# First batch's coarse softmax scaled inside its transposing matmul, second batch's sums moved from GpSimd to VectorE, and new queue orders

## The chip, the cores and the metric

The kernel runs on one core of a Trainium2 chip. The metric is the device time of one execution in microseconds, taken as the median of several runs. Engines are named as in the profile: PE is TensorE (PEld its weight loads), DVE is VectorE, ACT is ScalarE, POOL is GpSimd, SP is SyncE, which issues the DMAs.

## The reference

Four batches of 576 positions go through three stages: a two-scale attention, a block with a two-dimensional Fourier transform and an MLP, and a gated output block.

```python
# attention, per batch and head (8 heads, head size 64, factor 4, S = 576, Sd = 144)
out_d = sm_attn(q_d, k_d, v_d)            # q_d.. are means over groups of 4 positions
out_up = np.repeat(out_d, 4, axis=2)      # the coarse part, "base" in the kernel
mask = np.abs(pos[:, None] - pos[None, :]) < 4
scores = np.where(mask, 0.125 * q @ k.T, -1e9)
out_local = softmax(scores) @ v
x = out_up + out_local                    # reshaped to (4, 576, 512)
# Fourier and MLP
u = x + real(fft(fft(x, axis=1), axis=2))
un = (u - mean) / sqrt(var + 1e-6)
y = u + relu(un @ w_ch1) @ w_ch2          # 512 -> 2048 -> 512
# gate
gate = sigmoid(5-tap causal convolution of y along the sequence)
out = (gate * (y @ w_val)) @ w_out
```

## The kernel before, in words

Features lie on partitions and positions on the free axis: a batch's `X` is 128 x 4 x 576 (four feature blocks). The MLP and the gate work in 12 units of 192 positions (`UT`), three to a batch. Products of the main part are split into a high and a low float16 half (`uh`, `ul`, `hh`, `hl`), three matmul passes for one product; unit (0, 0) alone runs in float32 (`steps32`, tiles `u`, `h`), from weights as they arrive.

The weights arrive as 64-bit floats. For each piece of 1024 columns, DVE builds the float32 words in three integer operations (`word_op`, tiles `W`, `raw`), later ACT and DVE split them into halves (`conv_w`).

`chain0` is the head of the program: the attention and Fourier stage of batch 0. Its names in the rows are: `dS` scores of the local attention, `dmx` their maxima, `dP` the exponentials, `dsu` their sums, `dPT` and `PT` the transposed probabilities, `dO` the local output; `qkT` the pooled q and k, `sc` the coarse scores of a head pair, `nm` their maxima, `E` the coarse exponentials, `lsu` their sums, `eT` and `ET` the transposed probabilities, `po` and `base` the coarse output; `cv`, `tr`, `ss_v` and `tot` a norm of v; `fF`, `FH`, `FL` the folded sequence and its halves, `ab`, `AH`, `AL` the first Fourier product, `pp`, `pq`, `DS` the second. `mir` is a mirrored copy. The head ends with `u`, the centred input of unit (0, 0); the first matmul of the MLP (`ph` from `u`, line 1160) waits for it. Batches 1 to 3 do the same stage in `attn_steps`, spread between the units of the batch before; batch 1 needs its result at the fourth unit.

The coarse step of `chain0` for one head pair is `coarse` (PE), `coarse_max` (DVE), `coarse_exp` (ACT), `coarse_norm` (the sum plus 1e-9 and its reciprocal on DVE, then the product of the exponentials with it on GpSimd), `coarse_turn` (eight 72 x 72 transposes on PE into `eT`, a copy to `ET` on ACT) and `coarse_value`.

The order of the work is fixed by hand: `ORDER` lists, for SP and the four engines, in which sequence the numbered steps of the program (`parts`) stand in that engine's queue, and each queue runs strictly in that order. `SLOT` says which buffer of a ring each tile takes. `EN_G`, `XB_G` and the expressions in `attn_steps` choose between GpSimd and another engine for single operations.

Of the kernel before, what the change touches and what calls it, by code (L numbers as in the profile page):

```python
# [9 lines left out]
F32 = mybir.dt.float32  # L10
# [9 lines left out]
SD = S // 4  # L20
# [34 lines left out]
0 2 1 4 7 3 5.0 11 5.1 6 13 9 8 14 10 15.2 12 15.1 16.0 15.3-4 195.1 16.1 15.0 119.2 15.5 119.3 185.0 123.1 16.2 119.0  # L55
123.0 119.1 122.1 195.0 122.0 171 172.0 170 174 172.1 173 211.1 211.0 229.1 229.0 185.1 230.1 185.2 230.0 284 308.1
285 309.1 288.1 262.0 288.0 262.1 310.0 262.2 289.1 289.0 271 309.0 308.0 359 324 360.0 310.1 360.1 310.2 361.1 361.0
420.1 341 362.1 345 362.0 386.1 386.0 421.0-1 377 386.2 403 472.0 419.0 472.1 421.2 420.0 419.1 459 475 476 477.1 446
477.0 487 512.1 547 512.0 512.2 532 528 565 606 595 625 654 664 687 690 691
""",  # L60
    "gpsimd": """
0.0 5 48.1 48.0 54 71 85 136.1 136.0 137 139.1 139.0 0.1 195.1 195.0 195.2 183.0-1 183.3 183.2 193 211.1 211.0 229
211.2 217.0-1 217.3 230.1 217.2 230.0 230.2 231 241.1 241.0 249 255 259.1 259.0 267 269 272.1 272.0 274.1 274.0 275
277.0 286.0-2 283.0 286.3 283.1-5 290.0 283.6 290.1 283.7 290.2 283.8 121 278.0 290.3 286.4 277.1 318 278.1 339 359.1
325.1 325.0 390.0 359.0 337 307 359.2 360.1 360.0 361.1 361.0 360.2 361.2 390.1 362 390.2-3 395 398 404.0 408.1 408.0
407.1 407.0 404.1 411 428.1 428.0 434.0 417 414.1 414.0 434.1 483.0-1 472.1 472.0 472.2 451 475.1 475.0 475.2 476
# [50 lines left out]
197.8 213.0 209 197.15 204 210 197.16 193.2 214 219 215 212 213.2 213.1 220 216.0-2 250 251 221 216.3-4 216.9-10 216.5
216.11 216.6-7 222 216.8 216.12 217 236.0-1 216.13-16 224 231.0 225 231.3-5 231.1-2 236.2 226 252.1 257 252.0 236.3
# [1812 lines left out]
```

## Time and profile before

| | before |
|---|---|
| median of 3 runs | 667.07 us (666.96 to 668.61) |
| the profiled execution, its own time | 668.18 us |
| its span, first to last instruction | 666.4 us |
| PE busy | 647.4 us, 97% of the span |
| PE weight loads busy | 581.6 us |
| DVE busy | 458.3 us, 69% |
| ACT busy | 328.5 us, 49% |
| POOL busy | 127.1 us, 19% |
| mean granted TensorE clock | 0.985 of full speed |

The time of an execution is the span and some 1.8 us around it. A busy PE is not PE at its peak, since matmuls overlap one another; a clock of 0.50 in a row is TensorE at 1.2 GHz, one of 1.00 is 2.4 GHz.

### The profile page before, as it was taken

The numbers are of one execution on the slowest core, as the hardware profiler recorded it, in microseconds if no ns is written. First come the engines' busy times: TensorE is split into PE (matmuls) and PEld (weight loads), VectorE is DVE, ScalarE is ACT, GpSimd is POOL, SyncE is SP. The second block draws the span as 40 slices with busy tenths as digits, with TensorE's granted clock in tenths as the row PEclk, the third lists the DMA queues.
The fourth block names the chain that finished last, engine by engine and source line by source line (L and its number), as shares of the span: only waits on it lengthen the run. The fifth ranks groups of instructions, "written<-read, shape, count | busy, mean of one in ns | idle before, by whom it ended". The sixth has DMA issues, their size and how long they took to land.

```text
span 666.4 us, 18165 instructions
## 1 busy us (share of the span) xinstructions
PE 647.4 (97%) x7751; PEld 581.6 (87%) x7751; DVE 458.3 (69%) x950; ACT 328.5 (49%) x997; POOL 127.1 (19%) x178
## 2 busy tenths in 40 slices
PE   8968999999999999999999999999999999999997
PEld 4647799999998887989988898998999989999895
DVE  3679999989998877657876645675447763562344
ACT  3665577888334757675235576643232313312122
POOL 0240306321210613501110352030001020000000
PEclk9959999999999999999999999999999999999999
DMA  8976072313424001403240020000300000000001
GB/s 301 402 247 243 2 253 82 101 34 100 161 60 171 20 18 46 142 1 104 77 150 2 27 62 17 3 1 25 116 2 17 2 1 33 1 2 18 2 32 48
DMA packets 23299, 52.08 MB, mean 78 GB/s; under 512 B 1855, under 2 KB 11071, under 8 KB 22194
## 3 DMA queue, kind: packets, MB, share of 16 engines
q1 hardware_dynamic: 23218, 50.91, 22.4%
q8 instruction: 61, 1.00, 0.6%
q14 instruction: 20, 0.16, 0.1%
HBM read 44.41 MB, written 8.26 MB: 79 GB/s over the span
## 4 chain that ended last, share of the span: by engine, by line
PE 78%; DVE 11%; issue 5%; DMA 3%; POOL 2%; ACT 1%; SPq 0%; POOLq 0%; ACTq 0%
PE ph L1196 25%; PE pc L1216 24%; PE out L1324 7%; PE val L1308 7%; DVE W L448 5%; PE ab L996 2%; POOL E L451 1%; PE dO L805 1%; PE po L1572 1%; PE st L1080 1%; PE sc L883 1%; DMA raw<-in_moe_w_ch_dram 1%; PE pc L1171 1%; DMA kTa<-in_k_dram 1%; PE dPT L788 1%
## 5 line engine op out<-in xcount | busy, mean ns | idle before, releaser
L1196 PE MATMUL ph<-uh,W 128*128 128x192 f16 x1408 | 198.3, 246 | 1.3 <-DVE hl L448 0.7
L1196 PEld LDWEIGHTS <-W 128*128 128x128 f16 x2112 | 176.8, 98 | 9.5 <-issue 4.3
L1216 PE MATMUL pc<-hh,W 128*128 128x192 f16 x1232 | 171.7, 246 | 0.0
L1196 PE MATMUL ph<-ul,W 128*128 128x192 f16 x704 | 171.2, 246 | 0.0
L1216 PEld LDWEIGHTS <-W 128*128 128x128 f16 x1848 | 154.3, 98 | 5.7 <-issue 1.4
L1216 PE MATMUL pc<-hl,W 128*128 128x192 f16 x616 | 129.5, 246 | 0.0
L1200 ACT ACTIVATE hh<-ph 128x384 f16<-128x384 f32 x88 | 42.7, 488 | 125.8 <-PE ph L1196 100.5
L448 DVE SCALAR_TENSOR_TENSOR hl<-ph,hh 128x384 f16<-128x384 f32 x88 | 48.2, 552 | 77.6 <-ACT hh L1200 77.4
L448 DVE SCALAR_TENSOR_TENSOR W<-X,cw,W 128x192 f32<-128x192 f32 x160 | 64.1, 437 | 2.7 <-ACT W L1271 2.3
L1308 PE MATMUL val<-yy,W 128*128 128x192 f16 x576 | 59.6, 246 | 0.5 <-ACT yy L1250 0.5
L1308 PEld LDWEIGHTS <-W 128*128 128x128 f16 x576 | 48.5, 98 | 1.1 <-issue 0.4
L1324 PE MATMUL out<-W,gh 128*128 128x512 f16 x144 | 46.5, 379 | 0.0
L769 ACT ACTIVATE dP<-dS,dmx 128x64 f32<-128x64 f32 x120 | 36.2, 329 | 0.6 <-PE dPT L788 0.3
L448 DVE SCALAR_TENSOR_TENSOR W<-W,W 128x1024 int32<-128x1024 int32 x24 | 29.5, 1237 | 0.1
L451 POOL TENSOR_TENSOR E<-E,lsu 72x288 f32<-72x288 f32 x16 | 18.9, 1197 | 55.1 <-ACT nm L1529 19.7
L454 POOL TENSOR_TENSOR sq<-sq 128x384 f32<-128x384 f32 (+1 forms) x12 | 10.6, 880 | 93.6 <-ACT sq L1091 93.2
L1324 PE MATMUL out<-W,gl 128*128 128x512 f16 x72 | 27.1, 379 | 0.0
L769 ACT ACTIVATION_READ_ACCUMULATOR dP<-dS,dmx 128x1 f32 x120 | 26.7, 223 | 0.0
L1324 PEld LDWEIGHTS <-gh 128*128 128x128 f16 x144 | 14.0, 98 | 12.0 <-issue 0.2
L1216 PE MATMUL pc<-hh,Wz 128*128 128x192 f16 x176 | 24.3, 246 | 0.0
L1171 PE MATMUL pc<-h,W 128*128 128x192 f32 x128 | 23.3, 329 | 0.0
L1160 PE MATMUL ph<-u,W 128*128 128x192 f32 x128 | 22.5, 327 | 0.4 <-DVE u L1711 0.4
(288 smaller groups left out, 1212.0 us busy)
## 6 DMA issues: line engine op xcount, KB each, us to landing
W<-in_moe_w_ch_dram SPq DMA_DIRECT2D x12, 1024.0 KB
out_dram<-osb SPq DMA_DIRECT2D x17, 256.0 KB
vw<-in_vw_dram SPq DMA_DIRECT2D x8, 512.0 KB
v<-in_vp_dram SPq DMA_DIRECT2D x24, 144.0 KB
X<-in_q_dram SPq DMA_DIRECT2D x6, 576.0 KB
kT<-in_k_dram SPq DMA_DIRECT2D x4, 582.0 KB
X<-in_moe_w_ch_dram SPq DMA_DIRECT2D x2, 1024.0 KB
raw<-in_moe_w_ch_dram SPq DMA_DIRECT2D x4, 512.0 KB
```

The source lines that it names most:

```text
L448: return eng.scalar_tensor_tensor(out=out, in0=in0, scalar=scalar, in1=in1, op0=op0, op1=op1)
L451: return eng.tensor_tensor(out=out, in0=a, in1=b, op=ALU.mult)
L454: return eng.tensor_tensor(out=out, in0=a, in1=b, op=ALU.add)
L769: A.activation(out=s_[:, z, a], in_=pss[par][:, z, a], func=AF.Exp, scale=SCALE, bias=mx[:, par, z, a:a + 1], accum_out=su[:, par, z, a:a ...
L996: T.matmul(out=ps[0:n, c0:c1], lhsT=d[x][:, c, sd, e, n0:n0 + n], rhs=feat[:, w, c, c0:c1], start=(t == 0), stop=(t == 5),)
L1160: T.matmul(out=ps[:, e], lhsT=W[AT[kc * 2 + m // 8] + 1][:, o:o + 128], rhs=u()[:, kc, :], start=(kc == 0), stop=(kc == 3))
L1171: T.matmul(out=c["ps"][m // 2][:, m % 2], lhsT=W[9 + g][:, o:o + 128], rhs=hs[g // 2][:, g % 2, e, :], start=(kk == 0 and m % 2 == 0), sto ...
L1196: T.matmul(out=ps[:, e], lhsT=w1_ap(pw, kc, 2 * g + e), rhs=uh[px][:, kc, :], start=(t == 0), stop=(t == 11))
L1200: A.activation(out=h_, in_=ps, func=AF.Relu)
L1216: T.matmul(out=ps[m // 2][:, m % 2], lhsT=w2_ap(pw, kk, m), rhs=x[px][:, e, :], start=(kk == 0 and (pw, px) == (0, 0) and m % 2 == 0), sto ...
L1308: T.matmul(out=ps[:, e], lhsT=wv_ap(pw, kc, 2 * mh + e), rhs=m_["y"][px][:, kc, :], start=(t == 0), stop=(t == 11))
L1324: T.matmul(out=ps, lhsT=(gh, gl)[px][:, kc, t * 128:(t + 1) * 128], rhs=wo_ap(pw, kc), start=(n == 0), stop=(n == 11))
```

## The change

Six things change.

1. `coarse_norm` of batch 0 no longer multiplies the exponentials on GpSimd. DVE builds, for each head pair and head, a 72 x 2 x 72 tile `dg`: the unit matrix with the reciprocal sums on its diagonal. `coarse_turn` multiplies by it in a plain float32 matmul where it transposed by the unit matrix. Eight DVE operations take the place of eight GpSimd operations.
2. `EN_G` is empty: batch 1's coarse exponentials are scaled by ACT (16 operations of 72 x 144) where GpSimd did it in 8.
3. `XB_G` is gone: two base additions of batch 1 go from GpSimd to DVE.
4. Batch 1's two differences `fs` and its four far-half additions (`X<-X,DS`, 128 x 287) go from GpSimd to DVE.
5. The tile `busy`, whose products fill waits of PE at the start, shrinks to 128 x 128 and is read four times over for the same 512 columns.
6. `ORDER` is new for all five queues, and `SLOT` for two rings; of both a line or two stand below.

```diff
-EN_G = (1,)
+EN_G = ()
-XB_G = ((1, 1), (1, 3))
...
-    busy = const.tile([P, 512], F16, name="busy")
+    busy = const.tile([P, P], F16, name="busy")
...
-                add(G if (b, a) in XB_G else V, x[:, a], x[:, a], d["base"][:, a].unsqueeze(2).to_broadcast([P, SD, 4]))
+                add(V, x[:, a], x[:, a], d["base"][:, a].unsqueeze(2).to_broadcast([P, SD, 4]))
...
-                    (V, G)[sd].tensor_tensor(
+                    (V, G)[sd * (b > 1)].tensor_tensor(
...
-                add(G, X[:, c, b0:b1], X[:, c, b0:b1], DS[:, 1, HALF - 2:0:-1])
+                add(V if b == 1 else G, X[:, c, b0:b1], X[:, c, b0:b1], DS[:, 1, HALF - 2:0:-1])
...
-                add(G, X[:, c + 2, b0:b1], X[:, c + 2, b0:b1], DS[:, 0, HALF - 2:0:-1])
+                add(V if b == 1 else G, X[:, c + 2, b0:b1], X[:, c + 2, b0:b1], DS[:, 0, HALF - 2:0:-1])
...
             for par in range(2):
-                mul(G, E[:, par], E[:, par], s_[:, par].unsqueeze(2).to_broadcast([QC, 2, SD]))
+                lr["dg", a, par] = sp.tile([QC, 2, QC], F32, tag="dg", name="dg", bufs=3)
+                mul(V, lr["dg", a, par], eye[0:QC, 0:QC].unsqueeze(1).to_broadcast([QC, 2, QC]),
+                    s_[:, par].unsqueeze(2).to_broadcast([QC, 2, QC]))
...
-                        T.transpose(out=pe[:, kc, qc], in_=lr["E", a][:, par, qc, kc * QC:(kc + 1) * QC],
-                                    identity=eye[0:QC, 0:QC])
+                        T.matmul(out=pe[:, kc, qc], lhsT=lr["E", a][:, par, qc, kc * QC:(kc + 1) * QC],
+                                 rhs=lr["dg", a, par][:, qc], start=True, stop=True)
```

The first place where the order moves is DVE's queue in the head, just ahead of the first `dsu` of the two large groups of local scores. Before, after the last reciprocal of `lsu`, it reads:

```order
L1540 RECIPROCAL lsu<-lsu 72x4
L547 TENSOR_SCALAR W_114<-X 128x1024
L547 TENSOR_SCALAR W_115<-W_123 128x1024
L448 SCALAR_TENSOR_TENSOR W_114<-X,W_114 128x1024
L448 SCALAR_TENSOR_TENSOR W_115<-W_123,W_115 128x1024
L547 TENSOR_SCALAR W_116<-W_119 128x1024
L448 SCALAR_TENSOR_TENSOR W_114<-X,W_114 128x1024
L448 SCALAR_TENSOR_TENSOR W_116<-W_119,W_116 128x1024
L1467 TENSOR_SCALAR dsu<-dsu 128x16
```

Now:

```order
L1548 RECIPROCAL lsu<-lsu 72x4
L523 TENSOR_REDUCE f_v_565<-tot 128x1
L459 TENSOR_TENSOR dg<-eye,lsu 72x144 x2
L555 TENSOR_SCALAR W_117<-W_120 128x1024
L525 TENSOR_SCALAR f2s_v_567<-f_v_565 128x1
L456 SCALAR_TENSOR_TENSOR W_116<-W_118,W_116 128x1024
L456 SCALAR_TENSOR_TENSOR W_115<-W_123,W_115 128x1024
L555 TENSOR_SCALAR W_117<-W_121 128x1024
L1475 TENSOR_SCALAR dsu<-dsu 128x16
```

The two `dg` products stand right behind the reciprocal, and four word operations instead of seven stand between them and `dsu`; more words stand earlier, so that 15 of them are ahead of this `dsu` where 11 were.

The second place is PE's queue in the head, from the second head pair on. Before:

```order
L1518 MATMUL sc<-qkT 72x144 x4
L1558 MATMUL po<-ET,vr 64x144
L1549 MATMUL eT<-eye,E_498 72x72
L1558 MATMUL po<-ET,vr 64x144 x3
L1549 MATMUL eT<-eye,E_498 72x72
L509 MATMUL tot<-ss_v_461,ones 128x1
L1549 MATMUL eT<-eye,E_498 72x72 x6
L1558 MATMUL po<-ET,vr 64x144 x4
L1549 MATMUL eT<-eye,E_551 72x72 x8
L1558 MATMUL po<-ET,vr 64x144 x4
```

Now:

```order
L1526 MATMUL sc<-qkT 72x144 x4
L1559 MATMUL eT<-dg,E_502 72x72 x8
L1568 MATMUL po<-ET,vr 64x144 x4
L517 MATMUL tot<-ss_v_465,ones 128x1
L1559 MATMUL eT<-dg,E_557 72x72 x8
L1568 MATMUL po<-ET,vr 64x144 x4
```

The same matmuls stand in nearly the same order, with `dg` in the place of `eye`.

The third place is DVE's queue at batch 1's folds, some 200 operations further on. Before, with the other two `fs` and two of the four base additions on POOL:

```order
L970 TENSOR_TENSOR fs<-X 128x577
L448 SCALAR_TENSOR_TENSOR tap<-X,cw,tap 128x192
L975 TENSOR_TENSOR fF<-fs 128x289 x2
L448 SCALAR_TENSOR_TENSOR tap<-X,cw,tap 128x192
L501 TENSOR_SCALAR p2b<-p2a 128x1
L448 SCALAR_TENSOR_TENSOR hl<-ph,hh 128x384
```

Now, from the third base addition on:

```order
L462 TENSOR_TENSOR X<-X,base 128x576
L456 SCALAR_TENSOR_TENSOR hl<-ph,hh 128x384
L456 SCALAR_TENSOR_TENSOR tap<-X,cw,tap 128x192
L462 TENSOR_TENSOR X<-X,base 128x576
L509 TENSOR_SCALAR p2b<-p2a 128x1
L978 TENSOR_TENSOR fs<-X 128x577
L983 TENSOR_TENSOR fF<-fs 128x289
L456 SCALAR_TENSOR_TENSOR tap<-X,cw,tap 128x192
L456 SCALAR_TENSOR_TENSOR hl<-ph,hh 128x384
```

All four base additions and all four `fs` stand in this queue, among the `hl` operations for which the MLP's second product waits.

## Rows read from the trace of the kernel before

**Rows 1.** Windows: start:end, length, busy us (instructions) by engine, PEclk, DMA share, GB/s.

```profile
31.00:42.00 11.00, 5.53 (x33) 3.64 (x33) 9.13 (x15) 5.51 (x31) 10.18 (x4) 0.53 1.03 383
42.00:52.00 10.00, 9.46 (x122) 7.52 (x121) 7.24 (x20) 7.58 (x39) 0.00 (x0) 0.50 0.36 72
52.00:79.00 27.00, 24.15 (x282) 19.18 (x280) 26.11 (x47) 16.49 (x35) 5.12 (x13) 1.00 0.42 151
79.00:200.00 121.00, 120.07 (x1402) 115.10 (x1403) 116.29 (x207) 79.78 (x232) 32.82 (x40) 1.00 0.32 109
200.00:250.00 50.00, 48.59 (x615) 43.14 (x613) 41.85 (x76) 29.58 (x86) 15.81 (x31) 1.00 0.20 69
250.00:640.00 390.00, 390.00 (x4788) 357.98 (x4786) 230.06 (x530) 165.62 (x490) 59.59 (x81) 1.00 0.12 36
```

**Rows 2.** PE's waits: for what, us in total, times, longest.

```profile
PE eT L1549 <- POOL E L451: 4.5, 1, 4.5
...
PE ph L1196 <- DVE hl L448: 0.7, 1, 0.7
```

**Rows 3.** Timeline of POOL in the head: start, us, [idle before <-releaser].

```profile
21.12 1.29 POOL L451 TENSOR_TENSOR E<-E,lsu 72x288 f32<-72x288 f32 x2 [19.67 <-ACT nm L1529]
...
34.42 7.30 POOL L451 TENSOR_TENSOR E<-E,lsu 72x288 f32<-72x288 f32 x2 [0.54 <-DVE lsu L1540]
```

**Rows 4.** Timeline of PE in the head.

```profile
27.63 0.71 PE L1558 MATMUL po<-ET,vr 72*64 72x144 f32 x8
29.04 0.67 PE L1549 MATMUL eT<-eye,E 72*72 72x72 f32 x8 [0.70 <-ACT base L1560]
...
41.15 1.32 PE L1549 MATMUL eT<-eye,E 72*72 72x72 f32 x8 [4.50 <-POOL E L451]
```

**Rows 5.** Timeline of ACT in the head.

```profile
41.88 0.41 ACT L1552 ACTIVATE ET<-eT 72x288 f32<-72x288 f32 x1 [4.58 <-PE eT L1549]
```

**Rows 6.** DVE's waits.

```profile
DVE dsu L1467 <- ACT dP L1462: 4.2, 1, 4.2
...
DVE tr L451 <- PE cv L1585: 2.6, 1, 2.6
...
DVE nm L1525 <- PE sc L1518: 2.4, 3, 1.2
...
DVE dmx L1452 <- PE dS L1439: 1.0, 2, 0.9
```

**Rows 7.** Windows of 1 us where the granted clock falls and rises.

```profile
31.00:32.00 1.00, 0.82 (x6) 0.38 (x5) 1.00 (x3) 0.51 (x3) 1.00 (x2) 0.84 1.00 327
...
52.00:53.00 1.00, 0.88 (x16) 0.65 (x16) 1.00 (x2) 1.00 (x2) 0.00 (x0) 0.92 0.06 16
```

**Rows 8.** Groups of DVE by line and form: busy us, mean ns, idle before.

```profile
L448 DVE SCALAR_TENSOR_TENSOR W<-W,W 128x1024 int32<-128x1024 int32 x24 | 29.5, 1237 | 0.1
...
L454 DVE TENSOR_TENSOR X<-X,base 128x576 f32<-128x576 f32 x10 | 7.4, 750 | 5.7 <-ACT base L932 5.7
...
L970 DVE TENSOR_TENSOR fs<-X 128x577 f32<-128x577 f32 x6 | 4.5, 751 | 0.3 <-ACT X L951 0.3
...
L454 DVE TENSOR_TENSOR uc<-uc 128x192 f32<-128x192 f32 x4 | 1.4, 353 | 0.1
...
L454 DVE TENSOR_TENSOR X<-X,DS 128x287 f32<-128x287 f32 x2 | 0.9, 456 | 0.0
...
L451 DVE TENSOR_TENSOR tr<-cv,eye 128x128 f32<-128x128 f32 x1 | 0.3, 291 | 2.6 <-PE cv L1585 2.6
```

**Rows 9.** Group of ACT by line and form.

```profile
L906 ACT ACTIVATE E<-E,lsu 72x144 f32<-72x144 f32 x32 | 11.5, 406 | 3.0 <-DVE lsu L901 2.0 <-DVE p2a L499 0.5 <-DVE lsu L900 0.4
```

**Rows 10.** Timeline of DVE: its first operation, and the one that ends the head.

```profile
9.07 1.35 DVE L1510 TENSOR_REDUCE qkT<-X 128x288 f32<-128x1152 f32 x1 [9.07 <-DMA X<-in_q_dram]
...
77.99 0.95 DVE L1711 TENSOR_TENSOR u<-X,st 128x768 f32<-128x768 f32 x1 [0.40 <-PE st L1707]
```

More of the change, by code (lines that the diff above doesn't have):

```diff
@@ new lines @@
+229.1 229.0 217.0-1 211.2 286.0 229.2 217.2 121 230.1 230.0 217.3 230.2 272 274.1 274.0 275.1 275.0 283.0 286.1-3
+283.1 286.4 283.2-4 290.0 283.5 290.1 283.6 290.2 283.7 290.3 283.8 318.1 318.0 339 325 359.1 359.0 359.2 337.1 337.0
+360.0-1 390.0-1 361.1 361.0 361.2 360.2 362.0-1 417 362.2 390.2-3 395 398 404 407 408 411.0 428.0 307 428.1 411.1
+414.1 434 414.0 483.0 472 475.1 475.0 451 483.1 475.2 476.1 476.0 476.2 483.2-3 477 530.0-1 519 530.2-3 523 529.0 534
+529.1 537.1 537.0 538 543 593 623
@@ new lines @@
+127.7-9 127.13-15 127.24 127.10-11 127.16-18 127.25-35 127.19-23 126.2-3 141.0-5 142.0 142.9-12 142.1 142.13-14
+142.2-8 142.15-17 141.6-8 148.0-6 148.9 148.7 148.10 148.8 148.11-17 151 183 158 192.1 192.0 192.2 192.4 161 162 192.6
+192.3 192.5 192.7 192.9 192.8 192.10 192.12 192.14 192.11 192.13 192.15 192.17 192.16 184 193.0 191 166 193.1-3
+194.0-2 196 194.3-5 207.0 218.2-3 218.0-1 218.4 218.6 218.5 218.7 194.6-7 197.1 197.0 197.2-27 197.29 197.28 197.30-33
+207.1-6 200.0 193.4-7 200.1-4 213.0-2 207.7 200.5-7 223.0 223.2 223.1 223.3 223.6-7 223.4-5 210.0-3 213.3 227.0
@@ new lines @@
+461.16 461.18 466.3-5 460.4-5 461.19-23 451.0-31 451.33 451.32 468.0-1 466.6-7 460.6-23 461.17 466.8-23 463 464.0
+464.6-7 464.1-3 464.8-9 464.4-5 464.12 464.10 464.13 464.11 464.18-19 464.14-15 464.20-21 464.16 464.22-23 464.17
+465.0-7 467.6-8 467.0 467.9 467.1-3 467.10 467.4-5 467.11 467.18 467.12 467.19-20 467.13 467.21 467.14-16 467.22-23
+467.17 468.2-9 465.8-9 465.12 465.10 465.13 465.16 465.11 465.14 465.17 465.20-21 465.15 465.18-19 465.22-26 465.28
+465.27 465.29-36 465.38-39 465.37 468.10-23 470.0-2 470.6-8 470.3-5 470.12-13 470.9-11 470.14 470.18 470.15-16
@@ new lines @@
+493.16-17 493.21-23 504.0-13 491.4-6 491.0-3 491.7 499.13-23 491.8-11 504.14-23 501.6 501.0 501.7 501.1-4 501.8-9
+501.5 501.10-11 501.18-19 501.12-14 501.20 501.15 501.21 501.16 501.22-23 495 501.17 509.0-13 508.0 508.6-8 508.1
+508.9-10 508.2 508.11 496.0 496.4-6 496.1-3 496.7 514.0-5 497.1 497.0 497.2-3 496.8-11 509.14-18 514.6-23 508.3
+508.18-19 508.4-5 508.12 508.20 508.13-14 508.21 508.15 508.22-23 508.16-17 511.0-1 511.6 511.2 511.7 511.3 511.8
+509.19-23 511.9-11 511.18-19 511.4-5 511.12-14 511.20 511.15 511.21 511.16 511.22 511.17 511.23 500.0 500.4 500.1
@@ new lines @@
+500.5-7 500.2 502.0-1 502.3 502.2 517.0-9 500.3 515.6 515.0-4 515.7 515.5 515.8-11 515.18 515.12 515.19 515.13
+515.20-21 515.14 515.22 515.15 515.23 524.0 515.16-17 518.0 500.8-11 517.10-23 518.6 518.1-3 518.7-11 518.18 518.4-5
+518.12 518.19-20 518.13 518.21-22 518.14-16 524.1-12 505.0-1 505.4 505.2 505.5-7 505.3 524.13-20 518.17 518.23 526.0
+505.8-11 520.0-3 520.6 520.4-5 520.7-8 520.12 520.9-11 520.13-14 520.18-23 524.21-23 520.15-17 507.0-7 510.0-3
+526.1-14 535.0-9 507.8 535.10-12 526.15-23 534.0 531.6 507.9 531.0 531.7 531.1 510.4-5 531.2 510.6-16 531.8-9 531.3
@@ new lines @@
+507.10-14 535.13 507.15-18 529.0-1 535.14-17 507.19-23 510.17-18 531.10 531.4-5 531.12-14 531.11 531.18-19 531.15
+531.20-21 531.16-17 531.22-23 529.2 535.18-21 530.0 539.0-2 539.6 539.3 535.22-23 510.19-22 542.0-7 510.23 539.7-9
+539.4-5 539.12 539.10-11 539.13 539.18-19 539.14-15 539.20 539.16-17 539.21-22 532.0-2 544.0 542.8-23 539.23 530.1
+529.3-4 546.0 534.1 544.1-3 544.6 544.4 544.7-8 544.5 546.1-6 534.2-5 550.0 544.9 544.12 544.10-11 544.18-19 544.13
+550.1-2 529.5 546.7-9 529.6 544.20-21 544.14-15 547.0-2 532.3-5 544.16 544.22 550.3 532.6-7 534.6 529.7 550.4-15
@@ new lines @@
+639.6-14 636.11-14 642.21 642.16 642.22 642.17 642.23 651.0 649.0-3 651.1-3 649.4 644.0 644.6-7 644.1-3 644.8-9
+644.4-5 644.12-14 644.10 644.15 644.11 644.18-19 644.16 644.20 644.17 644.21-23 636.15-16 639.15-17 649.5-23 645.0
+645.6 645.1 645.7 645.2 645.8-9 645.3-5 645.10-13 645.18-21 645.14 645.22 645.15-16 645.23 645.17 639.18 636.17-18
+651.4-12 639.19 651.13-18 653.0 653.6 653.1 653.7-8 653.2-4 636.19-20 651.19-23 656.0-18 653.5 653.12 636.21-23
+653.13-14 660.0-7 653.15 656.19-21 653.9-10 653.16 653.11 653.18 639.20-22 656.22 639.23 653.17 653.19-23 660.8-23
@@ L296 @@
+667.16-17 654.10-11 667.22 668.3-15 667.23 670.2-8 674.0-1 668.16-23 670.9-23 669.0 669.6 669.1-5 669.12-13 669.7-11
+669.14-15 669.18-21 669.16-17 669.22-23 671.6-8 671.0-1 671.9-10 671.2-5 671.11-12 671.18-22 671.13-17 671.23 672.0
+672.12 672.1-11 672.13-23 674.2-16 675.0-8 674.17-18 675.9-23 685.0-3 688.0-2 674.19-23 689.0-13 688.3-23 685.4
+689.14-23 687 690 691
 """,
@@ L1417, in fill @@
                 for _ in range(n):
-                    T.matmul(out=ps, lhsT=busy[:, 0:P], rhs=busy, start=True, stop=True)
+                    T.matmul(out=ps.rearrange("p (a c) -> p a c", c=P), lhsT=busy, rhs=busy.unsqueeze(1).to_broadcast([P, 4, P]), start=True, stop=True)
         def score(g):
```

433 lines of the change are left out of this document (203 added, 230 removed), and 3 rows, old and new, of the table ORDER.

## The prediction, made before the changed kernel ran

> **What bounds the kernel now.** I read the windows first [rows 1]. From 79 us to 200 us PE is busy for 120.07 of 121 us, and from 250 to 640 us for 390.00 of 390; only 200 to 250 leaves 1.4 us. The first matmul of the MLP follows `u`, which DVE ends at 77.99 + 0.95 = 78.94 us [rows 10]. From there to the end of the span, 666.4 us, PE has 587.4 us of work with almost no gap, and the change leaves these matmuls as they are (the MLP, the gate and three batches' attention). So time is won or lost in two ways only: `u` comes earlier or later, or PE waits behind it.
>
> In the head, ahead of `u`, PE is not the bound: 5.53 of 11 us between 31 and 42, at half clock from there to 52 [rows 1]. DVE is. Its rows between 52 and 79 read 26.11 of 27 us, and it has waits only before that: 4.2 us at `dsu` for ACT's `dP`, 2.6 us at `tr`, 2.4 us at `nm`, 1.0 us at `dmx` [rows 6]. What makes `dsu` late is a chain over four engines. POOL's product of the second head pairs, L451, takes 7.30 us from 34.42 on, while the same two operations at 21.12 took 1.29 [rows 3]; PE's `eT` at 41.15 has waited 4.50 us for the later of the two [rows 2, 4]; ACT's copy at 41.88 has waited 4.58 us for `eT` [rows 5], and `dP`, behind it in ACT's queue, is late for DVE by 4.2 us. One slow GpSimd operation is thus handed on from engine to engine nearly in full.
>
> From 79 to 200 us DVE is busy too, 116.29 of 121 us, so it has 4.7 us left there; between 200 and 250 it has 8.15 us, and from 250 on 160 us [rows 1]. This matters for edits 3 and 4.
>
> **The change, part by part.** *Edit 1, in the head.* It removes eight GpSimd products and with them the releaser of PE's 4.50 us. In DVE's queue two `dg` stand right behind each reciprocal, so `eT` can run as soon as PE is there. Recovered on DVE: the 4.2 at `dsu`, whose cause is gone. The waits at `tr` (2.6) and `nm` (2.4) are for PE, which was early enough only by the old order; the new queue has 15 word operations ahead of the first `dsu` where 11 stood, so there is work to put into them, and I count both as filled. The 1.0 at `dmx` is at the first scores, ahead of any word, and I leave it. That is 4.2 + 2.6 + 2.4 = 9.2 us, with 4.2 and 10.2 as the ends.
>
> The edit costs DVE eight `dg`, 72 x 144, two inputs, float32, one of them broadcast. No row of before has it. The nearest are `tr`, 128 x 128 with 291 ns, and `uc`, 128 x 192 with 353 ns [rows 8]; 144 lies near the first, so 0.30 each and 2.4 in all, with 2.3 and 2.8 as ends. On PE a transpose becomes a float32 matmul. Eight rows of `po<-ET,vr`, which are float32 matmuls of 144 columns, took 0.71 us, and eight transposes of 72 columns 0.67 [rows 4]. There are 32, in four head pairs of eight; if each went twice through PE as these do, that would be up to 0.67 more a pair, 2.7 in all. PE has 5.5 us idle between 31 and 42 to hide it, so it costs 0; without that cover it would delay `ET` by 0.67 a pair.
>
> *The head's start.* DVE began with a `qkT` of 1.35 us at 9.07 us [rows 10], while it waited for the first scores; now a `dmx` comes first, so that this work may lie behind the wait. It costs 0 to 1.35; I take half, 0.65.
>
> The head together: 9.2 - 2.4 - 0.65 = 6.15 us earlier.
>
> *Edit 2.* Sixteen ACT products of 0.406 us [rows 9] are 6.5 us, in a stretch in which ACT is busy 79.78 of 121 us [rows 1]. I take 0; if ACT were late its copies and `hh` would be next, and after them PE. On the other side, eight POOL products no longer make anything wait. GpSimd's share of that stretch (32.82 us) is loose, and a gain through it is bounded by PE's few waits.
>
> *Edits 3 and 4.* DVE gets two base additions of 0.750, two `fs` of 0.751 and four far halves of 0.456 [rows 8]: 1.5 + 1.5 + 1.82 = 4.8 us. They lie ahead of batch 1's second Fourier product and its first unit, which PE needs some 150 us after the MLP began, and queued behind them are `hl` operations, for which PE waits. DVE's 4.7 us and, later, 8.15 us of idle time are the cover [rows 1]. In order, some of it shows: I take 0.5 us, bounds 0 and 4.8. Against it stands what PE waited for before, 0.7 us at `hl` [rows 2], which a new order may remove; I take 0.5 of it back. Body: 0, from -0.7 to +4.8.
>
> *Edits 5 and 6.* The `busy` products have the same 512 columns and stand ahead of the first scores, where PE waits for data: 0. What `ORDER` moves is in the parts above; before the first matmul of the MLP PE's work is the same in both.
>
> The sum, against the profiled execution's 668.18 us (its span of 666.4 and 1.8 around it): 668.18 - 6.15 = 662.0. That execution stands 1.1 us above the median of the runs, 667.07, so the forecast for the median is 667.07 - 6.15 = 660.9, said as 661.0.
>
> A rule speaks against the part on PE. The Trainium skill, "Perfetto Trace Analysis", section "Transposes", asks that logical transposes be done in transpose mode and not by a standard matmul, since the mode skips arithmetic. By that rule alone, with the doubled price of before on the path, it would be 661.0 + 2.7 = 663.7; no row of before shows this matmul with `dg`.
>
> **The rivals.** *A: the clock stays up as well.* The granted clock falls to 0.84 in the window from 31 and is back at 0.92 only in that from 52 [rows 7], after PE had worked for about half of the time. With the 4.50 us wait gone the fall may not come. PE's 9.46 us between 42 and 52 would then take 4.7 [rows 1]. If all of this reached `u` it would give 661.0 - 4.7 = 656.3; if half, 658.6. For it: without the wait PE works more densely between 31 and 42. Against: the clock had begun to fall at 31, before the wait (36.65 to 41.15), and DVE's word operations, not PE, fill most of 42 to 52. The Trainium skill, "TensorE: Matmul & The Clock Gate", section "Part 4: PE-mode transpose", states that transposes don't count as PE-busy in the same way for the clock; by that rule matmuls in their place would speak for A. The rows cannot tell.
>
> *B: the wait only changes its name.* `dg` stands in DVE's strict queue among word operations of 1.24 us [rows 8]. If each of four pairs waits for one of them, that is 4.9 us, about what POOL cost, and `dsu` still waits for ACT, which does the exponentials of both attentions. Then 1.2 us or less of the 6.15 is left, or 3.6 if half of the pairs wait: 663.5 to 667. For it: ACT and DVE are both used in 31 to 42, DVE 9.13 of 11 us. Against: `dg` is right behind the reciprocal.
>
> *C: slower, DVE becomes the bound behind `u`.* Its added work up to 200 us is 2.4 + 4.8 = 7.2 us. If the head's waits come back under the new order, the 2.4 us lie on the path to `u`; the 4.8 us meet 4.7 us of idle time from 79 to 200 [rows 1], of which, in a strict queue, little may be usable, and reach PE through `hl`. That gives 667.07 + 2.4 + 0.1 = 669.6 with all the idle time used and 674.3 with none. It decides when the head recovers less than 0.5 us with that time used, less than 5.2 without. For it: DVE is at 96% there. Against: the unit that needs this work comes late, and the cause of the 4.2 us is certainly removed. That the change doesn't do what it says is excluded only for the edits of engine, whose rows the order shows; whether a `dg` is fast is not.
>
> **How the numbers follow.** The sum's own range: 10.2 - 2.3 gives 7.9 in the head and 0.7 in the body, 658.5; half of `tr` and `nm` lost gives 663.5. It has a chance of 0.52, A 0.22, B 0.17, C 0.09. A measurement of this kernel can tell about 0.3%, 2.0 us: faster is below 665.1, slower above 669.1. The first two are faster, of B about 0.05 is; the rest of B (0.12) and 0.01 of C are the same, 0.08 slower. The range goes from A's end with 0.7 of the body, 655.6, said as 656, to the end of B with a little body, 667.5; what is left out is C, and a piece of A's end with the head's full 7.9 us.
>
> **What would show it.** Right: no `E` products on POOL in the head, PE's 4.50 us before `eT` gone, DVE's wait before `dsu` under 1 us, `u` at about 72 us and `ph` from `u` at 73, `dg` near 0.30 us. The body: from `ph` to the end 587 us, and PE's waits at `hl` not above 1 us, with DVE busier from 73 to 194 by some 4 us. A would show as 1.00 in windows from 31 to 52. B as `eT` waiting for `dg`, or `dsu` still waiting for `dP` by 3 us or more. C as `hl` waits of several us in batch 0's units. The forecast is wrong if the start of DVE's or SP's new order brings data later than the head can use, or if the filled waits at `tr` and `nm` come back.

## The result, and the profile after

The changed kernel takes 661.99 us, median of 4 runs (661.83 to 662.26), against 667.84 (666.96 to 669.71) of the kernel before on the same chip: ratio 0.9909, 95% interval 0.9885 to 0.9933. The forecast was 661.0, from 656 to 667.5. The profiled execution takes 661.96 us, its span is 660.2.

`u` and the first matmul of the MLP behind it, in the timelines of DVE and of PE (start, us, ..., idle before and its releaser):

```profile
73.52 0.95 DVE L1721 TENSOR_TENSOR u<-X,st 128x768 f32<-128x768 f32 x1 [0.36 <-PE st L1717]
```

```profile
74.53 1.73 PE L1168 MATMUL ph<-u,W 128*128 128x192 f32 x9 [0.45 <-DVE u L1721]
```

`u` starts 4.47 us earlier than in [rows 10], so `ph` starts at 74.53 and not at 79.00. From there to the end of the span PE needs 660.2 - 74.53 = 585.7 us, where it was 587.4. So 4.5 us came in the head and 1.7 behind it: both terms moved, in opposite directions, from a forecast of 6.15 and 0.

For the head, one window from DVE's first large operation to the end of `u`, in the kernel before and then in the changed one:

```profile
9.07:78.94 69.87, 58.99 (x706) 44.36 (x706) 57.62 (x112) 43.71 (x175) 17.88 (x21) 0.85 0.70 253
```

```profile
10.55:74.47 63.92, 57.66 (x674) 43.83 (x666) 59.04 (x120) 43.39 (x173) 5.07 (x13) 0.92 0.74 263
```

DVE was idle for 69.87 - 57.62 = 12.25 us and is now for 63.92 - 59.04 = 4.88: 7.37 recovered. It is busy 1.42 us longer, and it starts 1.48 later. 7.37 - 1.42 - 1.48 = 4.47, all of the head. Its waits in the head, as in [rows 6]:

```profile
DVE dmx L1460 <- PE dS L1447: 10.8, 2, 10.6
DVE DS L456 <- ACT qs L1685: 2.1, 1, 2.1
DVE X L462 <- PE dO L1503: 0.7, 2, 0.4
DVE dsu L1475 <- ACT dP L1470: 0.5, 1, 0.5
DVE nm L1533 <- PE sc L1526: 0.4, 2, 0.2
```

The 4.2 at `dsu` is gone: the 0.5 that stands there belongs to an earlier, smaller `dsu` (at 15.67 us). The 2.4 at `nm` is 0.4, and `tr` is gone from the list. The 10.8 at `dmx` is almost all the wait for the first data. New is 2.1 at `DS`, near the end of the head. PE's waits (compare [rows 2]), the third of which explains it:

```profile
PE eT L1559 <- DVE dg L459: 1.6, 1, 1.6
PE po L1568 <- ACT ET L1562: 1.6, 2, 1.2
PE pq L1675 <- POOL AH L1669: 1.3, 1, 1.3
...
PE ph L1204 <- ACT uh L1132: 0.5, 1, 0.5
```

And POOL at that place:

```profile
63.88 0.10 POOL L1669 MEMSET AH<- 97x1 f16 x1 [62.76 <-DVE AL L456]
63.91 0.10 POOL L1670 MEMSET AL<- 97x1 f16 x1
64.05 2.71 POOL L462 TENSOR_TENSOR vr<-v 72x256 f32<-72x256 f32 x1
66.70 0.09 POOL L1670 MEMSET AL<- 96x1 f16 x1
66.74 0.09 POOL L1669 MEMSET AH<- 96x1 f16 x1
66.77 0.10 POOL L1395 MEMSET X<- 128x16 f32 x1
66.82 0.09 POOL L1669 MEMSET AH<- 96x1 f16 x1
```

`vr`, an addition for batch 1 that nothing waits for here, now stands between the first zeroing of `AH` and the other two. It takes 2.71 us, so these two, of one column each, come only at 66.74 and 66.82. PE's `pq` waits for the first of them, ACT's `qs` for `pq`, DVE's `DS` for `qs`. In the kernel before, `vr` stood behind the zeroings (the last of them at 71.00):

```profile
71.09 2.47 POOL L454 TENSOR_TENSOR vr<-v 72x256 f32<-72x256 f32 x1
```

The stages after, as in [rows 1]:

```profile
31.00:42.00 11.00, 8.09 (x76) 6.39 (x75) 10.86 (x25) 9.67 (x58) 0.00 (x0) 0.79 1.02 373
42.00:52.00 10.00, 9.13 (x181) 7.96 (x174) 9.32 (x20) 3.97 (x16) 0.00 (x0) 0.72 0.76 194
52.00:73.00 21.00, 19.58 (x181) 15.20 (x180) 18.59 (x35) 15.18 (x31) 3.84 (x9) 1.00 0.36 130
73.00:194.00 121.00, 120.55 (x1435) 115.68 (x1435) 110.52 (x209) 85.27 (x249) 16.42 (x34) 1.00 0.35 120
```

Two things stand out. The granted clock is 0.79 and 0.72 in the first two windows, where it was 0.53 and 0.50. And from 73 to 194, a window of the same length as 79 to 200 before, DVE is busy for 110.52 us where it was 116.29, although edits 3 and 4 gave it 4.8 us more to do.

### The profile page after: what moved, and what is told of

It reads as the page before. It is cut to its first block, busy times and chain, and to the rows that moved or that the text cites. A ratio compares the mean times of both kernels' runs of the same rounds, so it can differ in the third digit from the quotient of the medians.

```text
span 660.2 us, 18206 instructions
## 1 busy us (share of the span) xinstructions
PE 647.8 (98%) x7783; PEld 582.5 (88%) x7783; DVE 450.6 (68%) x966; ACT 334.2 (51%) x1013; POOL 92.9 (14%) x154
## 4 chain that ended last, share of the span: by engine, by line
PE 65%; DVE 1%; ACT 1%; issue 0%; ACTq 0%
PE pc L1224 22%; PE ph L1204 21%; PE out L1332 7%; PE val L1316 7%; PE ab L1004 1%; PE dO L813 1%; PE st L1088 1%; PE po L936 1%; PE sc L891 1%; PE pp L1027 1%; PE pq L1027 1%; PE eT L926 1%; PE dS L763 1%; PE dPT L796 1%; PE pn L1027 0%; DVE ul L1133 0%
## 5 line engine op out<-in xcount | busy, mean ns | idle before, releaser
L1204 PE MATMUL ph<-uh,W 128*128 128x192 f16 x1408 | 201.1, 246 | 0.5 <-ACT uh L1132 0.5
L1224 PE MATMUL pc<-hl,W 128*128 128x192 f16 x616 | 127.2, 246 | 0.0
L1316 PE MATMUL val<-yy,W 128*128 128x192 f16 x576 | 61.9, 246 | 0.0
L1224 PE MATMUL pc<-hh,Wz 128*128 128x192 f16 x176 | 25.9, 246 | 0.0
L1224 PEld LDWEIGHTS <-Wz 128*128 128x128 f16 x264 | 22.2, 98 | 0.7 <-issue 0.5
```

The lines of the kernel that those rows point to most:

```text
L1204: T.matmul(out=ps[:, e], lhsT=w1_ap(pw, kc, 2 * g + e), rhs=uh[px][:, kc, :], start=(t == 0), stop=(t == 11))
L1224: T.matmul(out=ps[m // 2][:, m % 2], lhsT=w2_ap(pw, kk, m), rhs=x[px][:, e, :], start=(kk == 0 and (pw, px) == (0, 0) and m % 2 == 0), sto ...
L1316: T.matmul(out=ps[:, e], lhsT=wv_ap(pw, kc, 2 * mh + e), rhs=m_["y"][px][:, kc, :], start=(t == 0), stop=(t == 11))
```

## The experiments

Theory after the result: GpSimd's work is the cause in both parts. In the head its product is late for PE; behind `u` it makes PE wait and slows DVE. Rival: the new order is the gain, whoever does the work. The third question is what the new wait at `DS` costs.

All runs, each against the kernel before on the same chip; `ph` is the start of the first matmul from `u` in the profile, "behind" the time from there to the end of the span:

| run | median us | ratio to before, 95% | `ph` | behind |
|---|---|---|---|---|
| before | 666.70 to 667.84 | 1 | 79.0 | 587.4 |
| changed, again | 661.86 | 0.9916 (0.9904 to 0.9929) | 74.4 | 585.5 |
| zeroing ahead of `vr` | 659.87 | 0.9890 (0.9873 to 0.9908) | 71.9 | 585.6 |
| edits 2 to 4 undone | 664.83 | 0.9977 (0.9960 to 0.9995) | 74.8 | 588.2 |
| edit 2 undone | 663.31 | 0.9951 (0.9934 to 0.9968) | 73.6 | 587.1 |
| edit 1 undone | 663.38 | 0.9935 (0.9923 to 0.9948) | 75.8 | 585.9 |
| edit 1 undone, zeroing ahead | 663.93 | 0.9953 (0.9936 to 0.9970) | 76.7 | 586.0 |
| order alone | 666.72 | 0.9990 (0.9978 to 1.0002) | 75.6 | 588.8 |
| edit 1 alone | 663.50 | 0.9944 (0.9930 to 0.9959) | 75.1 | 586.5 |
| before, scaled by DVE | 664.78 | 0.9952 (0.9937 to 0.9968) | 74.8 | 586.4 |
| changed, scaled by DVE | 663.87 | 0.9948 (0.9936 to 0.9960) | 76.1 | 586.0 |
| the same, with matmuls | 663.20 | 0.9942 (0.9929 to 0.9956) | 75.4 | 586.0 |
| filler on PE | 664.38 | 0.9959 (0.9944 to 0.9974) | 76.6 | 585.5 |

A single profile's `ph` is good to about 1 us: the first `dmx` starts between 9.3 and 10.7 us from run to run, when its data have come. And the 587.4 of before belongs to an execution of 668.18 us, above all its medians; the same matmuls in the same order took 586.5 and 586.4 in the two runs on its order. Two profiles are of the fastest execution of their kernel: edit 2 undone (662.46, median 663.31) and before, scaled by DVE (663.01, median 664.78).

**The changed kernel again.**

> The changed kernel once more, beside the three that follow, so that differences of a few tenths of a per cent are read on one chip. Every theory: 662.0 us, 0.991 of before.

It took 661.86, as the first time.

**The new wait.** In GpSimd's order alone:

```diff
-5.1 5.0 0.0 136 195.1 137.1 137.0 0.1 139 195.0 183.0
+5.1 5.0 0.0 136 137.1 137.0 139 195.1 0.1 195.0 183.0
```

(195.1 is `vr`, 137 and 139 are the zeroings of the second and third block.)

> The changed kernel, with one edit in GpSimd's order: the four small zeroing operations of AH and AL of the second and third block stand ahead of batch 1's addition of v (vr) instead of behind it. In the changed kernel PE waits 1.3 us at pq for such a zeroing, which lies behind a vr of 2.71 us, and DVE then waits 2.1 us at DS. Theory: this wait sets the end of the head, so u comes 1.3 to 2 us earlier and the time is 660.0 to 660.7. Rival: the second Fourier product is late for another reason (the weight loads, or DVE's AL) and the time stays at 661.7 to 662.3.

659.87 us, 2.0 below the changed kernel beside it, and `u` 2.5 us earlier than there. DVE's wait at `DS`, and POOL in this run:

```profile
DVE DS L454 <- ACT qs L1683: 0.7, 1, 0.7
```

```profile
63.20 0.10 POOL L1668 MEMSET AL<- 96x1 f16 x1 [0.43 <-DVE AL L454]
63.23 0.10 POOL L1667 MEMSET AH<- 96x1 f16 x1
63.92 0.10 POOL L1667 MEMSET AH<- 96x1 f16 x1 [0.59 <-DVE AL L454]
63.96 0.10 POOL L1668 MEMSET AL<- 96x1 f16 x1
64.09 1.43 POOL L460 TENSOR_TENSOR vr<-v 72x256 f32<-72x256 f32 x1
```

The zeroings now wait only for DVE's `AL`, PE's wait at `pq` is gone, and the wait at `DS` is 0.7, 1.4 us less. The rest of the 2.5 us stands at `X<-dO`, whose wait is 0.7 and 1.4 us in the two profiles of the changed kernel and 0.2 here, so one profile does not tell whether it belongs to the zeroing. The new order had given back 1.4 to 2 us by one addition in the wrong place. By its median this version is the fastest of all; against the changed kernel the intervals just touch, and one of its five runs took 662.70.

**Edits 2 to 4 undone** (batch 1's scaling, base additions, `fs` and far halves on GpSimd; `ORDER` adapted, the rest of the new order kept):

```diff
-EN_G = ()
+EN_G = (1,)
-                add(V, x[:, a], x[:, a], d["base"][:, a].unsqueeze(2).to_broadcast([P, SD, 4]))
+                add(G if (b, a) in ((1, 1), (1, 3)) else V, x[:, a], x[:, a], d["base"][:, a].unsqueeze(2).to_broadcast([P, SD, 4]))
-                    (V, G)[sd * (b > 1)].tensor_tensor(
+                    (V, G)[sd].tensor_tensor(
-                add(V if b == 1 else G, X[:, c, b0:b1], X[:, c, b0:b1], DS[:, 1, HALF - 2:0:-1])
+                add(G, X[:, c, b0:b1], X[:, c, b0:b1], DS[:, 1, HALF - 2:0:-1])
...
```

> The changed kernel with edits 2 to 4 undone: batch 1's coarse exponentials scaled by GpSimd, two base additions, two fs and four far halves on GpSimd again, where the old order had them; the rest of the new order stays. Behind u the changed kernel is 1.7 us shorter than before. Theory A (the order gave this, the engines did not): within 0.5 us of the changed kernel, 661.5 to 662.5, with PE's waits behind u not above 1.5 us. Theory B (the moves from GpSimd gave it): 663.5 to 664, with waits at hl, uh or dO again. Theory C (the added DVE work costs time that the order hides only in part): faster than the changed kernel, 661 or less.

Theory B, and more than its 663.5 to 664: 664.83, and 588.2 us behind `u`, 2.6 more than the changed kernel. PE waits again behind `u`, above all for one of the products:

```profile
PE eT L922 <- POOL E L455: 1.7, 1, 1.7
...
PE ph L1200 <- ACT uh L1128: 1.0, 1, 1.0
```

Edits 2 to 4 are worth 2.6 us by the profiles and 3.0 by the medians under the new order; by the ratios it is 4, since five of this run's twelve executions took 666.6 to 668.9. The order in itself is no gain behind `u`: with the old engines (this run, and the order alone) it needs 588.2 and 588.8, more than the old order's 586.4 to 587.4.

**Edit 2 undone** (`EN_G` alone):

> The changed kernel with edit 2 alone undone: batch 1's coarse exponentials scaled by GpSimd in 8 products where ACT does it in 16; edits 3 and 4 stay. With edits 2 to 4 undone the run took 664.8 us and PE waited 1.7 us for such a product. Theory (edit 2 carries most of it): 663.3 to 664.2, PE waiting for E by 1 to 2 us. Rival (the base additions, fs and far halves carry it): 661.8 to 662.5.

663.31, 587.1 behind `u`, and the same 1.7 us of PE at `eT`. By the profile edit 2 carries 1.5 of the 2.6 us, edits 3 and 4 the other 1.1; by the ratios it is 2.3 and 1.7. I had priced edit 2 at nothing.

**Edit 1 undone, in the new order.**

```diff
-                lr["dg", a, par] = sp.tile([QC, 2, QC], F32, tag="dg", name="dg", bufs=3)
-                mul(V, lr["dg", a, par], eye[0:QC, 0:QC].unsqueeze(1).to_broadcast([QC, 2, QC]),
-                    s_[:, par].unsqueeze(2).to_broadcast([QC, 2, QC]))
+                mul(G, E[:, par], E[:, par], s_[:, par].unsqueeze(2).to_broadcast([QC, 2, SD]))
-                        T.matmul(out=pe[:, kc, qc], lhsT=lr["E", a][:, par, qc, kc * QC:(kc + 1) * QC],
-                                 rhs=lr["dg", a, par][:, qc], start=True, stop=True)
+                        T.transpose(out=pe[:, kc, qc], in_=lr["E", a][:, par, qc, kc * QC:(kc + 1) * QC],
+                                    identity=eye[0:QC, 0:QC])
```

> The changed kernel with edit 1 undone: the eight products of the coarse exponentials on GpSimd, transposes by the unit matrix, no dg on DVE; the new order of everything else stays. Theory (GpSimd's products, slow beside DVE's word operations, hold the head): products of several us again, PE waiting for E by 3 us or more, and the time 665 to 668. Rival (the new order gave the gain, whoever scales): 661.5 to 663.

663.38: between the two ranges, and nearer the rival's. GpSimd's products are slow again, and PE waits for them:

```profile
21.78 3.50 POOL L456 TENSOR_TENSOR E<-E,lsu 72x288 f32<-72x288 f32 x2 [20.66 <-ACT nm L1534]
26.59 1.76 POOL L456 TENSOR_TENSOR E<-E,lsu 72x288 f32<-72x288 f32 x2 [1.31 <-ACT ET L1557]
31.63 5.04 POOL L456 TENSOR_TENSOR E<-E,lsu 72x288 f32<-72x288 f32 x2 [3.29 <-DVE lsu L1545]
```

```profile
PE eT L1554 <- POOL E L456: 6.2, 5, 4.1
```

But DVE no longer pays all of it. In the head it waits:

```profile
DVE lsu L1544 <- ACT E L1539: 3.3, 1, 3.3
...
DVE DS L453 <- ACT qs L1680: 0.7, 1, 0.7
DVE dsu L1472 <- ACT dP L1467: 0.5, 1, 0.5
```

The 0.5 at `dsu` is again the earlier one, so with the products still on GpSimd the new order fills the 4.2 us there, at the price of 3.3 us at `lsu`. And here the wait at `DS` is 0.7, not 2.1: in this run `vr` took 0.72 us. It had ended (67.39) before DVE's next word operation began (67.68), while in the changed kernel such an operation (64.96 to 66.17) falls into its 2.71 us. So the comparison flatters GpSimd. To see by how much, the same with the zeroing ahead of `vr`:

> The changed kernel with edit 1 undone (products on GpSimd, transposes) and the four zeroing operations ahead of vr. With edit 1 undone alone the run took 663.4 us, where PE waits 6.2 us for the products but DVE only 0.7 us at DS, since vr took 0.72 us there and not 2.71. Theory (edit 1 is worth more than the 1.4 us that this comparison shows, because the changed kernel loses some 2 us to the zeroing behind vr and that run does not): no gain from the zeroing here, 663.0 to 663.6, and so 3 us or more above the changed kernel with the same edit (659.9). Rival (the zeroing is worth 2 us in every order): 661.0 to 661.6.

663.93, no gain, as the theory had it. Against 659.87 with edit 1 and the same zeroing, edit 1 is worth about 4 us in the new order (0.9953 against 0.9890), of which the changed kernel shows 1.5. In the profiles of these two, which begin alike (first `dmx` at 9.72 and 9.73), `ph` differs by 4.8.

**Edit 1 alone, and DVE's scaling alone, in the old order; the order alone.** The first is the kernel before with edits 1 and 5 (the smaller `busy` tile makes the room for `dg` in SBUF), the two `dg` right behind each reciprocal. The second scales `E` by `mul(V, ...)` at the same places and keeps the transposes. The third undoes edits 1 to 4 in the changed kernel, with the diffs shown above together.

> The kernel before with edit 1 alone (and edit 5, whose smaller tile makes the room for dg): dg on DVE right behind each reciprocal, the transposing matmul, nothing on GpSimd; all else in the old order. Theory (my sum): the 4.2 us at dsu go, the waits at tr and nm stay, 2.0 to 2.4 us of dg come on: 2 us faster than before, 664.5 to 666, and u at 76.5 to 77.5. Rival (the old order gives nothing back without being rewritten): no faster than before, 667 or more. Rival (the wait was all): 662.5 to 663.5.

> The kernel before, with the eight products of the coarse exponentials on DVE instead of GpSimd, right behind each reciprocal; transposes and order as before. Against the run before it this has transposes in place of matmuls and products of 72 x 288 in place of 72 x 144. Theory (leaving GpSimd counts): 664.5 to 666.5, u at 77 to 78. Rival (the matmul counts): 667 or more.

> The kernel before with the new order alone: all work on the engines where it was before (edits 1 to 4 undone), all queues in the new order, the moved operations where the old order has them among their neighbours. Theory (edit 1 and the new order are worth their gain together in the head, the order gives the body's): u no earlier than 77.5 us, time 664.5 to 667. Rival (the order is the whole gain): 661.5 to 663. Rival (the order is written for the new engines and worse with the old): above 668.

Edit 1 alone takes 663.50, better than the sum had said and at the edge of the last rival's range, with `u` at 74.08. Its wait at `dsu` is gone, those at `nm` and `tr` stay, smaller by 0.2 and 0.5:

```profile
DVE nm L1524 <- PE sc L1517: 2.2, 3, 1.2
DVE tr L450 <- PE cv L1586: 2.1, 1, 2.1
```

DVE's scaling alone takes 664.78. The order alone takes 666.72, which is not told apart from the kernel before: `ph` comes 3.4 us earlier in the profile (`u` at 74.55, so the theory missed there), and 1.4 us are lost again behind `u`.

Do the gains of edit 1 and of the order add? One window from DVE's first large operation to the end of `u`, as above, in edit 1 alone, the order alone, and the changed kernel with the zeroing ahead:

```profile
8.07:75.03 66.96, 61.36 (x756) 46.72 (x753) 59.64 (x120) 43.73 (x175) 5.06 (x13) 0.90 0.72 268
10.57:75.50 64.93, 58.15 (x642) 42.95 (x634) 58.30 (x112) 43.27 (x173) 12.26 (x21) 0.84 0.74 260
9.73:71.79 62.06, 58.62 (x674) 44.84 (x666) 58.98 (x120) 43.38 (x173) 3.91 (x13) 0.89 0.78 275
```

DVE's idle time recovered less its busy time added, which leaves out when the first operation starts, is 4.93 - 2.02 = 2.9 us for edit 1 alone and 5.62 - 0.68 = 4.9 for the order alone, 7.8 together. The changed kernel has 7.37 - 1.42 = 6.0, and with the zeroing ahead it has 9.17 - 1.36 = 7.8. Both shorten the wait at `dsu` (order alone: 1.0 at the place of the 4.2), yet their gains add, within the 1 us of single profiles; what the changed kernel lacks is what the zeroing costs.

**Matmul or transpose.** The changed kernel with `E` scaled by DVE, once transposed, once multiplied by the unit matrix; the two differ in this line alone:

```diff
-                        T.transpose(out=pe[:, kc, qc], in_=lr["E", a][:, par, qc, kc * QC:(kc + 1) * QC],
-                                    identity=eye[0:QC, 0:QC])
+                        T.matmul(out=pe[:, kc, qc], lhsT=lr["E", a][:, par, qc, kc * QC:(kc + 1) * QC],
+                                 rhs=eye[0:QC, 0:QC], start=True, stop=True)
```

> The changed kernel with the exponentials scaled on DVE in place (eight products of 72 x 288 where the eight dg stood) and transposed by the unit matrix as before. Theory (only leaving GpSimd counts): DVE pays some 0.2 us more for each of eight, PE 0.6 us less for each pair: 662 to 664. Rival (the matmul in place of the transpose matters, for PE's clock): the clock falls earlier than 37.7 us, and the time is 664.5 or more.

> As the run before it (exponentials scaled on DVE), but the transpose is a plain float32 matmul with the unit matrix. The two differ in PE's mode alone. Theory: PE has idle time for the doubled passes, so it is within 0.7 us of the run before it. Rival, clock: with matmuls the clock falls later and rises earlier, and it is 1 us or more faster than the run before it. Rival, price: the passes lie on the path and it is 1 to 2.7 us slower.

Windows of the run with transposes, then of that with matmuls:

```profile
29.00:36.00 7.00, 4.59 (x35) 3.38 (x36) 6.68 (x14) 5.23 (x27) 0.00 (x0) 0.54 1.02 400
36.00:50.00 14.00, 11.68 (x138) 9.40 (x138) 13.61 (x30) 9.29 (x52) 0.00 (x0) 0.50 0.93 286
```

```profile
29.00:36.00 7.00, 5.09 (x54) 3.93 (x52) 6.93 (x15) 5.69 (x30) 0.00 (x0) 0.98 1.04 403
36.00:50.00 14.00, 12.20 (x156) 10.26 (x156) 13.62 (x30) 9.32 (x49) 0.00 (x0) 0.52 0.97 282
```

With transposes the clock is at half from 29.6 us on, with matmuls from 35.7, six microseconds later; it is back at 50.1 and 49.3. The start alone is a weak sign: in runs with the same head as the changed kernel the clock falls between 32.2 and 37.7. The times are 663.87 (663.34 to 664.18) and 663.20 (662.20 to 665.42); 0.7 us between the medians, not told apart. So the mode goes with the clock, and the head hardly notices, since DVE sets its end. Both are slower than the changed kernel by 1.3 to 2.0 us: a DVE product of 72 x 288 takes 442 ns where `dg` takes 291, 1.2 us for eight.

**Filler on PE.** Twelve products of `busy` ahead of the fourth pair's `eT`:

```diff
+                if (a, par) == (3, 1):
+                    for _ in range(12):
+                        T.matmul(out=pe.rearrange("p k q c -> p (k q) c"), lhsT=busy[:, 0:QC],
+                                 rhs=busy[:, 0:QC].unsqueeze(1).to_broadcast([P, 4, QC]), start=True, stop=True)
```

> The changed kernel with twelve more products of the busy tile on PE, ahead of the fourth head pair's eT, where PE waits 1.6 us for dg (their result is overwritten). They keep PE at work up to the point at which the granted clock falls in the changed kernel (37.7 us; it is back at 47.3). Theory: DVE sets the head's end, so even where the clock stays up the time moves by less than 0.7 us: 661.3 to 662.7. Rival A of the prediction (the low clock still costs time): with the clock at 1.00 from 37 to 47 the head ends 2 to 4 us earlier, 658 to 660. If the clock falls all the same, this run tells nothing on that.

The clock fell all the same (0.50 from 37 to 40, and 0.53 from 44 to 51), so on the clock it tells nothing. It tells something else: the twelve took 2.99 us at half clock, the last `eT` came 1.9 us later, DVE's waits at `dsu` rose from 0.5 to 2.0 us, and `ph` came 2.1 us later; 664.38. At this one place the chain `eT`, `ET`, `dP`, `dsu` still has little slack: 1.5 of the 1.9 us reach `dsu`.

## Why the prediction was right, and where not

The sign, the time (661.0 against 661.99) and the range were right. The profiled execution was even forecast at 662.0 and took 661.96, but that is two errors that cancel: the head's term was 1.7 us too large and the body's 1.7 too small.

- **The chain from GpSimd's product to `dsu`** was read rightly: edit 1 alone removes the wait at `dsu`, and its `ph` comes 3.9 us earlier, 1.0 of which is data that came earlier. What the prediction didn't see is that the order shrinks this wait too, to 1.0 us, with the products still on GpSimd. That does no harm to the sum: the two still add.
- **"I count both as filled"** (`tr` and `nm`, 5.0 us): 4.6 filled. They are the order's part: with edit 1 alone 4.3 of them stay.
- **The price of `dg`**: 0.30 each, measured 291 ns, and 2.0 us in all rather than 2.4, since neighbours overlap. A word of 0.7 us moved behind `u`, so DVE's head is longer by only 1.42.
- **The start**: 0 to 1.35 lost, half taken; it was 1.48, a little outside. The first `dmx` came at 10.55 where it came at 10.59 before, with no `qkT` ahead of it.
- **What the sum didn't have** is the wait at `DS`. I had looked at PE's and DVE's queues, but not at POOL's past the removed products; the row of `vr` ahead of two zeroings stood in its new order. 7.37 recovered, not 9.2; with the zeroing mended 9.17 are recovered and the head gains 7.1 us in the profile.
- **Body, "0, from -0.7 to +4.8"**: the mis-sized term. Measured -1.7 in the profiles, -0.9 against the other two runs on the old order. Edits 3 and 4 were priced as 4.8 us more for DVE, and "DVE busier by some 4 us" stood as the sign: it is busy 5.8 us less. DVE's operations of before had themselves been slowed beside GpSimd's (below), and most of that the order alone undoes. PE's waits for `hl` (0.7) and `yy` (0.5) are gone. Edit 2 wasn't free either, but a gain: 1.5 us by the profile, under this order.
- **The price on PE** was rightly nothing: 16 records of `eT` took 1.2 to 1.3 us where 8 took 0.67 [rows 4], and 2.16 at half clock where 8 took 1.32, in PE's idle time; the run with matmuls was not slower than that with transposes. The Trainium skill's "Perfetto Trace Analysis", section "Transposes", would have had it the other way; the measurement decides, for this place.
- **Rival A** came true as a mechanism and not as a price. The clock's slow stretch was 20 us before and is 10 to 14 in every run with matmuls, and 17 to 20 in every run with transposes. The Trainium skill's "TensorE: Matmul & The Clock Gate", section "Part 4: PE-mode transpose", says that transposes don't count as PE-busy in the same way; the two runs that differ in the mode alone agree, with slow stretches of 20.5 and 13.7 us. The time was not A's 656.3 to 658.6, since DVE has 4.9 us of idle time in the whole head and PE's speed shows in little of it.
- **Rival B** is there once: `eT` waits 1.6 us for the fourth pair's `dg`, behind two word operations, and not 1.24 in each pair.
- **Rival C**: no `hl` wait, and DVE with more idle time, not less.

DVE's faster operations alone gain nothing behind `u`: the order alone has most of them and needs 588.8 us there. What goes with edit 2 is PE's wait of 1.7 us at `eT`. What stays open is how edits 3 and 4 bring the rest, and which queue of the new order, SP's with the transfers among them, brings its part of the head; none of these was undone by itself.

## What to carry to other kernels

A wait that one engine hands on to three others shrinks when any link is made early. Two edits that both touch it may still add, as here, so run each alone and both together, and first mend what became last: with the zeroing left where it was, the sum looked 2 us short. After a reordering, read every queue at the last chain ahead of the stage's end, also those of engines that hardly work: one addition on GpSimd between one-column zeroings cost 1.4 to 2 of nearly 8 us. And when work moves from GpSimd to VectorE, price it by the rows of both engines and by what runs beside it, since either slows the other.

## What the runs showed of the hardware

DVE's two-input operations and GpSimd's slow one another, both ways. For GpSimd it stood in [rows 3]: two products of one form take 1.29 us while DVE is at `nm` and `qkT`, and 7.30 beside its word operations. For DVE it is seen in the run with edits 2 to 4 undone. POOL's two `fs` there:

```profile
182.60 1.83 POOL L974 TENSOR_TENSOR fs<-X 128x577 f32<-128x577 f32 x1 [5.35 <-DVE fF L979]
185.86 1.49 POOL L974 TENSOR_TENSOR fs<-X 128x577 f32<-128x577 f32 x1 [1.43 <-DVE FL L452]
```

and DVE in the same microseconds:

```profile
181.00 0.69 DVE L452 SCALAR_TENSOR_TENSOR W<-raw,W 128x512 int32<-128x512 int32 x1
181.61 0.83 DVE L979 TENSOR_TENSOR fF<-fs 128x289 f32<-128x289 f32 x2
...
183.55 1.43 DVE L452 SCALAR_TENSOR_TENSOR W<-raw,W 128x512 int32<-128x512 int32 x1
...
185.64 2.03 DVE L979 TENSOR_TENSOR fF<-fs 128x289 f32<-128x289 f32 x2
...
187.77 0.83 DVE L979 TENSOR_TENSOR fF<-fs 128x289 f32<-128x289 f32 x2
```

Two `fF` take 0.83 us with GpSimd idle and 2.03 beside its `fs`; a word of `raw` 0.69 and 1.43. The Trainium skill's "GPSIMD Engine Reference", section "1. Specifications", states that GpSimd's way into SBUF is shared with VectorE, with contention where VectorE has two inputs in SBUF; these rows agree, and show that VectorE pays as well.

It matters which operations meet, and not only how long GpSimd works. From `ph` to the end of the span, before, with the order alone, and changed:

```profile
79.00:666.40 587.40, 581.32 (x7003) 534.31 (x7003) 400.66 (x839) 283.46 (x821) 108.23 (x151) 1.00 0.17 55
75.56:664.40 588.84, 581.43 (x7003) 534.18 (x7003) 394.31 (x839) 283.52 (x822) 108.97 (x151) 1.00 0.16 55
74.53:660.20 585.67, 580.75 (x7003) 534.17 (x7003) 391.51 (x847) 289.22 (x838) 87.21 (x135) 1.00 0.17 55
```

With the same 839 operations on DVE and the same 109 us on GpSimd, the order alone takes 6.3 us off DVE's busy time; the moves take off 2.8 more, although they add eight operations. Single operations show it: in the 121 us behind `ph` before, the 14 `tap` of the gate's convolution have a median of 0.41 us and a slowest of 1.75, beside a product and a base addition of GpSimd, and the four `FL` 0.82 and 1.97, beside its `fs`. In the changed kernel no `tap` there takes more than 0.42 us and no `FL` more than 0.82.
